# The second piece of wo as five transfers, and a small row built on GpSimd, in a decode kernel on one core

## The chip, the core and the metric

The kernel runs on one core of one Trainium2 chip. The time is device microseconds of that core for one execution. Each execution reads all inputs from HBM and writes 512 output numbers. The engines are TensorE (PE, with its weight loads as PEld), VectorE (DVE), ScalarE (ACT), GpSimd (POOL) and SyncE (SP, which issues nearly all transfers here). Sixteen DMA engines move the data.

## What is computed

One token passes through grouped-query attention with a long cache and through a gated feed-forward block; a sigmoid gate mixes the two results. All tensors are bf16. The shapes are: x 1x512, 32 query heads over 8 cache heads, 32768 cached positions of 128 numbers, feed-forward width 1792.

```python
g = _sigmoid((x * gate_w).sum(-1, keepdims=True))
# attention: q = x @ wq in 32 heads; k and v repeated 4 times
scores = jnp.einsum("bhqd,bhkd->bhqk", q, k) * (Dh ** -0.5)
p = _softmax(scores, axis=-1)
o = jnp.einsum("bhqk,bhkd->bhqd", p, v)
a = o.reshape(B, Sq, Hq * Dh) @ wo
# feed-forward: the same x
b = (_silu(x @ w_gate) * (x @ w_up)) @ w_down
return g * a + (1 - g) * b
```

The two caches are 134 MB of the 148 MB that are read; wq and wo are 4.2 MB each, and the three feed-forward matrices 1.8 MB each.

## The kernel before

**Storage.** `page` is five pages of 32 KB in each of the 128 partitions. One cache head of K or V fills two pages. wq first lies in page 3, the gate and up matrices in page 4; K uses pages 0 to 2 in turn (that of the first head 1 and 2), V pages 3 and 4, V of the last head pages 2 and 0. wo takes page 3 once V of the seventh head has been used there. Row `p` of the view of wo is partition `p`: it holds 32 rows of wo, `j` = 0 to 31, of 512 numbers (1 KB) each.

**The queue of transfers.** SP issues everything in program order (lines 310 to 329): wq, x, gate_w, gate, up, then K of head 0 in two halves, K of head 1 in two halves, V of head 0, K of head 2, V of head 1 and so on; then V of the last head in two halves, w_down, and wo. Several of these wait until a page is free: the second half of K of head 1 (line 289) waits until PE has transposed the first half of K of head 0, and wo (line 325) waits until V of the seventh head is used. What is queued behind a waiting transfer waits too. A load of 128 partitions is spread over the sixteen DMA engines, eight partitions to each.

**wo in pieces.** `WO_CUTS = [0, 16, 25, 29, 31, 32]` cuts wo by `j` into five pieces of 16, 9, 4, 2 and 1 rows per partition (2048, 1152, 512, 256 and 128 KB), each with a semaphore `sem_wo[k]`, so that PE can begin on a piece when it has landed. `emit_wo` (line 241) waits for a piece and multiplies its rows.

**The start.** PE begins with two small products (line 442) of a row of ones with `r_row`, the numbers 0 to 127 and their negatives; the difference is zero on the diagonal only, and DVE makes the identity matrix from it (line 622). `r_row` is built by DVE: a memset and seven additions (lines 606 to 614), each twice as long as the one before and each waiting for the last, and one multiplication by -1 (line 615). After line 442 PE waits for x (line 445), turns it into a column (line 448), and makes the queries (line 463) and the feed-forward products (line 501). Then the loop over the eight heads starts (line 533).

**The loop and the end.** In each turn PE transposes K in 16 units (line 337), DVE copies them out of PSUM (line 711), PE makes the scores (line 349), and the exponentials (ACT, line 586) and the product with V of the head before (line 406) follow. `emit_end` does the last head's V, the w_down product, and the first piece of wo (line 557, sixteen products at line 220). Behind the block, ACT copies their sum (line 762), PE adds it up in four column groups (line 757) and does the other four pieces of wo with `emit_rows` (line 231, four small products for each row `j`); DVE rounds the result (line 764), and two stores send it out.

**GpSimd** does two memsets of ones (lines 263 and 264), and then only adds to a semaphore (line 271) when pairs of K loads are in.

## Time and profile before

| what | value |
|---|---|
| median of 3 runs | 350.95 us (350.76 to 351.65) |
| profiled execution | 350.67 us |
| its span, first to last instruction | 349.3 us |
| mean granted clock of TensorE | 0.833 |
| PE, DVE, ACT, POOL busy | 75%, 54%, 10%, 0% of the span |
| bytes over the span | 148.11 MB read, 424 GB/s |

The profiled execution's own time is 1.37 us longer than its span. A busy PE is not a PE at its peak, since its products overlap. Three views are used: the page of the whole execution (busy time, the span in 40 slices, DMA queues, the chain of work that ended last); the instructions in order of time, where a bracket behind a row tells how long the engine idled before it and what ended that; and a table of stretches of time, with the busy time of each engine, the clock granted to TensorE and the mean busy share of the sixteen DMA engines in each.

### The profile page before, as it was taken

The page shows a single profiled execution, that of the slowest core. Times are in us where ns is not written, and L with a number is a line of the kernel's source. Part 1 is how long each engine was busy: PE and PEld are TensorE (multiplying, and loading weights), DVE is VectorE, ACT ScalarE, POOL GpSimd, SP SyncE. Part 2 cuts the span into 40 slices and gives each one's busy share as a digit, 9 for nine tenths or more (in the row PEclk, how much of TensorE's full clock was granted, in tenths as well). Part 3 has the DMA queues.
Part 4 walks back from the last instruction along what each step waited for, and adds up shares of the span by engine and source line. Part 5 has one row for each costly group of instructions (what it writes and reads, how often), then busy time and mean ns, then how long its engine had stood idle before and what let it go on. Part 6 is the DMA issues. An engine that isn't in the chain of part 4 may idle for free. (4 is left out here: it accounts for less than half of the span.)

```text
span 349.3 us, 8832 instructions
## 1 busy us (share of the span) xinstructions
PE 261.8 (75%) x3915; PEld 221.4 (63%) x3915; DVE 187.2 (54%) x236; ACT 33.4 (10%) x143; POOL 0.4 (0%) x6
## 2 busy tenths in 40 slices
PE   1354995899549980999669992999379983999484
PEld 1124994898349960997359942997279843995232
DVE  4144895698118931797139911796149811894110
ACT  1002000300210003000210003000400003000400
POOL 0000000000000000000000000000000000000000
PEclk9975898799858996799659986799859975998875
DMA  8999999999999999999999999999999999999995
GB/s 325 420 454 420 422 432 449 460 413 428 443 428 450 413 435 450 428 435 420 428 473 413 428 428 428 465 413 428 443 413 465 413 428 443 428 416 420 423 423 231
DMA packets 4051, 148.22 MB, mean 424 GB/s; under 512 B 458, under 2 KB 588, under 8 KB 844
## 3 DMA queue, kind: packets, MB, share of 16 engines
q1 hardware_dynamic: 4040, 148.12, 98.5%
q8 instruction: 6, 0.10, 0.1%
q14 instruction: 1, 0.01, 0.0%
q10 hardware_dynamic: 4, 0.00, 0.0%
HBM read 148.11 MB, written 0.00 MB: 424 GB/s over the span
## 5 line engine op out<-in xcount | busy, mean ns | idle before, releaser
L711 DVE COPY ktT<-pst 128x2048 bf16<-128x2048 bf16 x128 | 153.4, 1221 | 66.1 <-PE pst L337 62.1
L337 PE MATMUL pst<-ident_f,page 128*128 128x128 f32 x1024 | 148.7, 300 | 39.7 <-DMA page<-in_A_k_cache_dram 38.3
L337 PEld LDWEIGHTS pst<-ident_f,page 128*128 128x128 f32 x1024 | 127.2, 156 | 44.0 <-DMA page<-in_A_k_cache_dram 39.0
L349 PEld LDWEIGHTS ps_sc<-qcur,ktT 128*128 128x128 bf16 x2048 | 63.9, 97 | 8.1 <-DVE ktT L711 7.1
L349 PE MATMUL ps_sc<-qcur,ktT 128*128 128x8 bf16 x2048 | 64.2, 166 | 6.4 <-DVE ktT L711 6.4
L406 PE MATMUL ps_o<-page,ET 128*16 128x512 bf16 x512 | 38.2, 465 | 3.5 <-ACT ET L586 3.5
L406 PEld LDWEIGHTS ps_o<-page,ET 128*16 128x16 bf16 x512 | 14.1, 105 | 23.9 <-issue 12.1
L586 ACT ACTIVATE ET<-ps_sc,nbias 128x128 bf16 x64 | 23.9, 556 | 51.7 <-DVE nbias L737 51.7
L579 ACT ACTIVATE acc<-ps_o 128x512 f32<-128x512 f32 x8 | 4.8, 597 | 221.7 <-PE ps_o L406 217.6
L729 DVE TENSOR_REDUCE gm<-ps_m 4x1 f32<-4x128 f32 x8 | 2.2, 279 | 39.8 <-PE ps_m L386 39.8
L586 ACT ACTIVATION_READ_ACCUMULATOR ET<-ps_sc,nbias 128x1 f32 x64 | 18.3, 286 | 0.0
L719 DVE TENSOR_REDUCE pmaxf<-ps_sc 128x4 f32<-128x512 f32 x16 | 11.0, 686 | 8.4 <-PE ps_sc L349 8.4
L427 PE MATMUL ps_m<-sel,acc 128*128 128x4 f32 x64 | 8.4, 255 | 1.8 <-ACT acc L579 1.6
L427 PEld LDWEIGHTS ps_m<-sel,acc 128*128 128x128 f32 x64 | 7.7, 191 | 2.5 <-ACT acc L579 2.2
L390 PE MATMUL ps_m<-diag,ones_f 4*128 4x4 f32 x16 | 3.6, 294 | 6.8 <-DVE diag L733 6.8
L390 PEld LDWEIGHTS ps_m<-diag,ones_f 4*128 4x128 f32 x16 | 3.2, 245 | 8.4 <-issue 8.4
L696 DVE RECIPROCAL rS<-ps_m 128x4 f32<-128x4 f32 x9 | 1.6, 183 | 10.8 <-PE ps_m L427 10.8
L448 PE MATMUL ps_m<-ones_bf,x_row 1*128 1x1 bf16 x4 | 0.3, 172 | 9.3 <-DMA x_row<-in_A_x_dram 9.3
L418 PEld LDWEIGHTS ps_m<-esum,ones_f 128*128 128x128 f32 x32 | 4.2, 190 | 3.5 <-issue 3.5
L448 PEld LDWEIGHTS ps_m<-ones_bf,x_row 1*128 1x128 bf16 x4 | 0.2, 115 | 9.6 <-DMA x_row<-in_A_x_dram 9.6
L418 PE MATMUL ps_m<-esum,ones_f 128*128 128x4 f32 x32 | 4.9, 258 | 0.0
L764 DVE CAST res_row<-ps_sc 128x128 bf16<-128x128 f32 x1 | 0.3, 292 | 7.9 <-PE ps_sc L231 7.9
(70 smaller groups left out, 55.4 us busy)
## 6 DMA issues: line engine op xcount, KB each, us to landing
page<-in_A_k_cache_dram SPq DMA_DIRECT2D x4, 4096.0 KB, 34.4
page<-in_A_v_cache_dram SPq DMA_DIRECT2D x2, 4096.0 KB, 27.3
page<-in_A_wq_dram SPq DMA_DIRECT2D x1, 4096.0 KB, 13.5
page<-in_A_wo_dram SPq DMA_DIRECT2D x1, 2048.0 KB, 18.5
page<-in_B_w_gate_dram SPq DMA_DIRECT2D x1, 1792.0 KB, 16.7
page<-in_B_w_up_dram SPq DMA_DIRECT2D x1, 1792.0 KB, 20.6
wd<-in_B_w_down_dram SPq DMA_DIRECT2D x1, 1792.0 KB, 21.0
page<-in_A_wo_dram SPq DMA_DIRECT2D x1, 1152.0 KB, 21.0
```

What stands on the lines that cost most here:

```text
L337: ins = pe.transpose(pst[u % NST][:, k * 128 : (k + 1) * 128], kv[:, n * 128 : (n + 1) * 128], ident_f[:, :],)
L349: ins = pe.matmul(ps_sc[b][:, col : col + 2 * HPG], kt[:, k, e, :], qcur[:, e, :], start=(e == 0), stop=(e == 1),)
L390: pe.matmul(ps_m[:, M_B0 : M_B0 + HPG], ones_f[0:HPG, :], diag[:, :], start=True, stop=True,).then_inc(sem_b, STEP)
L406: ins = pe.matmul(ps_o[32 * c : 32 * c + RQ * HPG, :], ET[:, n : n + RQ, :].rearrange("p n h -> p (n h)"), v[:, k * RQ : (k + 1) * RQ, :], ...
L418: pe.matmul(ps_m[:, M_S0 : M_S0 + HPG], ones_f[:, :], esum[:, b, :], start=(b == 0), stop=(b == NB - 1),)
L427: ins = pe.matmul(ps_m[:, M_P0 : M_P0 + HPG], acc[:, q, :], sel4[:, q * HPG : (q + 1) * HPG], start=(q == 0), stop=(q == RQ - 1),)
L579: act.activation(part, ps_o[:, :], ACT.Copy).then_inc(sem_acc, STEP)
L586: act.activation(ET[:, b * R : (b + 1) * R, h], sc[:, h, bass.ds(bank, R)], ACT.Exp, bias=nbias[:, h : h + 1], scale=SCALE, accum_out=esum ...
L696: dve.reciprocal(rS[:, :], ps_m[:, M_S0 : M_S0 + HPG]).then_inc(sem_rs, STEP)
L711: dve.tensor_copy(ktT[:, n % NKT, :], pst[n % NST][:, :].bitcast(BF16)).then_inc(sem_cp, 1)
L719: dve.tensor_reduce(pmaxf[:, b, :], sc, AX.X, ALU.max).then_inc(sem_d, 1)
L729: dve.tensor_reduce(gm[:, :], ps_m[0:HPG, M_A0 : M_A0 + 128], AX.X, ALU.max).then_inc(sem_d, STEP - 2)
```

## The change

The second piece of wo (rows `j` = 16 to 24, 9 KB of each partition) becomes five transfers on the same semaphore: one of partitions 0 to 111, and four of four partitions each, 112 to 115, 116 to 119, 120 to 123 and 124 to 127. A transfer of 112 partitions gives each of sixteen DMA engines seven; one of four partitions is put on four of them. By the change's own words the same four engines take all four, so that they carry 11 rows of this piece and the other twelve 7, where each carried 8. PE waits for 80 counts in place of 16.

`r_row` is built by GpSimd, by the same nine operations, behind its two memsets; PE waits for the ninth count. In the built program one more instruction stands on GpSimd just ahead of its first addition: it loads the library of code that holds this operation. Nothing else moves on any engine.

```diff
+    ROW_CUTS = [(0, 112)] + [(n, n + 4) for n in range(112, 128, 4)]
...
         def emit_wo(pe, k):
-            pe.wait_ge(sem_wo[k], 16)
+            pe.wait_ge(sem_wo[k], 16 * len(ROW_CUTS) if k == 1 else 16)
...
             def _(pool):
                 pool.memset(ones_f[:, :], 1.0).then_inc(sem_ones, 1)
                 pool.memset(ones_bf[:, :], 1.0).then_inc(sem_ones, 1)
+                pool.memset(r_row[:, 0, 0:1], 0.0).then_inc(sem_r, 1)
+                n, k = 1, 1
+                while n < 128:
+                    pool.wait_ge(sem_r, k)
+                    pool.tensor_scalar(
+                        r_row[:, 0, n : 2 * n], r_row[:, 0, 0:n], float(n), None, op0=ALU.add
+                    ).then_inc(sem_r, 1)
+                    n *= 2
+                    k += 1
+                pool.wait_ge(sem_r, k)
+                pool.tensor_scalar(
+                    r_row[:, 1, :], r_row[:, 0, :], -1.0, None, op0=ALU.mult
+                ).then_inc(sem_r, 1)
...
                 for k, s in enumerate(sem_wo):
                     a, b = WO_CUTS[k], WO_CUTS[k + 1]
-                    sp.dma_start(wo_v[:, a:b, :], src[:, a:b, :]).then_inc(s, 16)
+                    for lo, hi in ROW_CUTS if k == 1 else [(0, 128)]:
+                        sp.dma_start(wo_v[lo:hi, a:b, :], src[lo:hi, a:b, :]).then_inc(s, 16)
...
                 def emit_start():
-                    pe.wait_ge(sem_dve_r, 1)
+                    pe.wait_ge(sem_r, 9)
...
-                dchain(dve.memset(r_row[:, 0, 0:1], 0.0))
-                n = 1
-                while n < 128:
-                    dchain(
-                        dve.tensor_scalar(
-                            r_row[:, 0, n : 2 * n], r_row[:, 0, 0:n], float(n), None, op0=ALU.add
-                        )
-                    )
-                    n *= 2
-                dve.tensor_scalar(
-                    r_row[:, 1, :], r_row[:, 0, :], -1.0, None, op0=ALU.mult
-                ).then_inc(sem_dve_r, 1)
                 dchain(dve.memset(qblk[:, :], 0.0))
```

More of the change, by code (lines that the diff above doesn't have):

```diff
@@ L94, in bass_gated_mix__gqa_block_cached__swiglu_ffn__decode_kernel @@
         sem_pz = S_("s_pz")
-        sem_dve_r = S_("s_dve_r")
+        sem_r = S_("s_r")
         sem_pe_d = S_("s_pe_d")
```

## The prediction

> **What bounds the kernel now.** First the page of the whole execution: the span, the DMA queues, the bytes.

> ```profile
> span 349.3 us, 8832 instructions
> q1 hardware_dynamic: 4040, 148.12, 98.5%
> q8 instruction: 6, 0.10, 0.1%
> q14 instruction: 1, 0.01, 0.0%
> HBM read 148.11 MB, written 0.00 MB: 424 GB/s over the span
> ```

> The data queue takes 98.5% of sixteen DMA engines over the span. No compute engine is near that, so only two things can change the time: bytes that arrive later, or the tail behind the last bytes. Seven packets are not data but instruction code (6 on q8, 1 on q14).

> Then the tail: the chain of work that ended last, and the DMA issues of wo with their time to landing.

> ```profile
> 344.52 0.61 ACT acc L762
> 345.12 0.04 issue
> 345.17 2.50 PE ps_sc L231 x72
> 347.67 0.02 issue
> 347.69 0.29 DVE res_row L764
> ```

> ```profile
> page<-in_A_wo_dram SPq DMA_DIRECT2D x1, 1152.0 KB, 21.0
> page<-in_A_wo_dram SPq DMA_DIRECT2D x1, 512.0 KB, 21.8
> page<-in_A_wo_dram SPq DMA_DIRECT2D x1, 256.0 KB, 22.0
> page<-in_A_wo_dram SPq DMA_DIRECT2D x1, 128.0 KB, 21.8
> ```

> ```profile
> L329 SPq DMA_DIRECT2D page<-in_A_wo_dram x5: 328/432/434, 323.7 to 325.5; - x5
> ```

> Issues run from 323.7 to 325.5, some 0.45 us apart, so the pieces land at about 345.1, 346.4, 347.0 and 347.3 us. Line 231 works through them to 347.67. Last, the tail in stretches of 0.2 us; the last two numbers of a row are the DMA engines' share and GB/s, the one ahead of them the granted clock.

> ```profile
> 344.60:344.80 0.20, 0.00 (x0) 0.00 (x0) 0.00 (x0) 0.20 (x1) 0.00 (x0) 0.50 1.06 405
> 345.00:345.20 0.20, 0.03 (x4) 0.04 (x5) 0.00 (x0) 0.11 (x1) 0.00 (x0) 0.50 0.78 292
> 345.20:345.40 0.20, 0.20 (x7) 0.18 (x11) 0.00 (x0) 0.00 (x0) 0.00 (x0) 0.50 0.49 190
> 346.00:346.20 0.20, 0.20 (x20) 0.20 (x12) 0.00 (x0) 0.00 (x0) 0.00 (x0) 0.50 0.38 138
> 346.40:346.60 0.20, 0.20 (x20) 0.20 (x13) 0.00 (x0) 0.00 (x0) 0.00 (x0) 0.50 0.32 108
> 346.60:346.80 0.20, 0.20 (x20) 0.20 (x15) 0.00 (x0) 0.00 (x0) 0.00 (x0) 0.50 0.12 41
> ```

> The share falls in two steps: to about half by 345.3, then it stays near 0.4 until 346.6. So some nine engines are done 1.3 to 1.5 us before the other seven, and a piece counts as landed when the last of the sixteen has put its part down. Seven late engines and seven packets of code fit each other: an engine that fetches code in mid-stream stays behind to the end, since all do equal work. Which engines are late no view tells.

> **The change, part by part: wo.** One row of the second piece on one engine: 1152 KB at 424 GB/s take 2.78 us, for eight rows on each engine, so 0.35 us a row. An engine with 7 rows is done 0.35 us earlier, in this piece and in the three behind it. One with 11 is done 3 x 0.35 = 1.05 us later.

> If the four are among the early nine, they end 1.05 us behind the early group, still at or before the late seven, who come 0.35 us earlier: the last piece lands at about 346.95 in place of 347.3. Of these 0.35 us PE can use only what it waits for:

> ```profile
> L231 PEld LDWEIGHTS ps_sc<-page,O 128*32 128x32 bf16 x64 | 1.8, 142 | 0.3 <-DMA page<-in_A_wo_dram 0.2
> ```

> Of its idle time 0.2 us was ended by a wo transfer. Otherwise it was busy from 345.17 on, at a granted clock of 0.50, and it started there because of line 762, that is of the first piece, which isn't touched. So the gain is between 0 (another engine is last) and 0.2 us; I take 0.15, since the row is rounded and PE's own pace is next behind it. If the tail's clock were full, up to 0.35 would come.

> SP issues four transfers more, 4 x 0.43 = 1.7 us from the same row. Ahead of the last data stand some 20 us of landing time, so nothing runs dry: 0. It costs something only if that queue were shorter than 4 us. The higher count on the semaphore moves no other wait on PE.

> Four transfers of 36 KB could each have a fixed price. The last piece, 128 KB, lands 0.45 + 21.8 - 22.0 = 0.25 us behind the one before (rounding makes it 0.15 to 0.4), and at 424 GB/s it takes 0.31. So a small transfer in a full queue costs at most 0.1 us more than its bytes: 0 to 0.4 us for four, nearest 0, which I take. [...]

> **The change: r_row on GpSimd.** DVE loses nine operations; its two PSUM memsets start some 1.7 us earlier, and nobody waits for them early. What matters is when r_row is ready. In order of time:

> ```profile
> 0.73 1.28 ACT L568 ACT_TABLE_LOAD   x1 [0.73 <-PEq L782]
> 0.87 0.10 POOL L264 MEMSET ones_bf<- 128x2 bf16 x1
> 0.89 1.34 DVE L610 TENSOR_SCALAR r_row<-r_row 1x1 f32<-1x1 f32 x7
> 1.17 0.32 SPq L311 DMA_DIRECT2D x_row<-in_A_x_dram  x1
> 2.53 0.79 PE L442 MATMUL ps_sc<-ones_f,r_row 1*128 1x128 f32 x2 [2.53 <-DVE r_row L615]
> 3.12 0.63 PE L442 MATMUL ps_sc<-r_row,ones_f 1*128 1x128 f32 x2
> 13.07 0.29 PE L448 MATMUL ps_m<-ones_bf,x_row 1*128 1x1 bf16 x4 [9.33 <-DMA x_row<-in_A_x_dram]
> 22.83 3.16 PE L501 MATMUL pst<-page,xT 128*1 128x448 bf16 x32 [1.79 <-DMA page<-in_B_w_up_dram]
> 44.66 0.33 SPq L290 DMA_DIRECT2D page<-in_A_k_cache_dram  x1
> ```

> Line 442 runs from 2.53 to 3.75, then PE idles 9.33 us for x. So r_row may be ready up to 13.07 - 1.22 = 11.8 us and nothing moves. Up to 1.8 us later line 501's wait for the up matrix takes it. Beyond that the first transposes come late, and with them the K load of 44.66, which they release. How much data is queued then:

> ```profile
> page<-in_A_k_cache_dram SPq DMA_DIRECT2D x1, 4096.0 KB, 17.1
> ```

> That load lands 17.1 us after its issue; its own bytes take 4096 KB / 424 GB/s = 9.9, so 7.2 are queue and start. Less 1.0 from issue to first data (the first transfer is issued at 0.73; the rows of the first two microseconds below) and less the 1.4 us by which early engines run ahead, some 5 us are spare.

> ```profile
> 0.00:1.00 1.00, 0.00 (x0) 0.00 (x0) 0.17 (x2) 0.27 (x1) 0.44 (x6) 1.00 0.00 0
> 1.00:2.00 1.00, 0.00 (x0) 0.00 (x0) 0.83 (x6) 1.00 (x1) 0.00 (x0) 1.00 1.34 360
> ```

> So r_row costs bytes only from about 11.8 + 1.8 + 5 = 18.6 us on, one for one.

> When is it ready? GpSimd is free at 0.97. DVE's chain steps every 0.19 us (1.34 / 7). GpSimd's step isn't in the trace; its memset of 0.10 us against DVE's 0.06 for a still smaller one speaks for about double, 0.4, and eight steps are 3.2 us. The load of code is not in the trace either. Bounds: 0, were the code there already, and 11.9 us, what a 1 KB transfer takes behind full queues (x: issued at 1.17, awaited at 13.07). Nearest in kind is ACT's load of a table, 1.28 us. Ready at 0.97 + 1.28 + 3.2 = 5.5 us, bounds 2.5 and 16.1: each of these below 18.6. I take 0. [...]

> **Sum.** wo -0.15, the rest 0: the profiled execution of 350.67 us (1.37 of it outside the span) would be 350.52. It stood 0.28 below the median of 350.95, so the median is put at 350.8.

> **The rivals.** (a) One of the four engines is late already. Then its 11 rows, not the seven rows of the rest, set the last landing. It decides from any lag over about 0.2 us behind the early group (1.05 + 0.2 is where the late seven now land, less 0.15 that PE absorbs), and lags are 1.3 to 1.5 or none. Price: the last landing 0.4 to 1.05 us later, as it is the first or last of the seven, and the tail behind it at full length: 351.35 to 352.0, middle 351.7. For it: seven of sixteen are late, and four drawn blindly would all be early in only some 7 of 100 cases. Against: code fetches that follow one another need not be spread blindly; if they sit side by side, four early neighbours are as likely as not.

> (b) r_row is later than 18.6 us, because its code needs two trips behind full queues, 2 x 11.9 us: ready at 0.97 + 23.8 + 3.2 = 28, so 9 us of missing DMA, 360. For it: x shows what a trip under load costs. Against: one trip is hidden, and the seven packets of code took 0.1% of the DMA engines between them.

> (c) The change doesn't do what it says: the four small transfers go to different engines, every engine is back at eight rows, 350.95.

> (d) The code of GpSimd comes through the same DMA engines as more packets like the seven, and DVE's shorter program saves one. A late engine hit twice adds 1.4 us: 352.3. One late engine fewer gains nothing while six remain.

> (e) A fixed price for small transfers, 0.4 us at its upper bound, on the four engines: inside the slack of early engines, so 350.95; this is a term of (a) more than a case.

> **How the numbers follow.** Forecast 0.45, (a) 0.30, (b) 0.10, (c) with (e) 0.07, (d) 0.08. This kernel's measurement tells a change from none at about 0.3%, 1.05 us: the forecast, (c) and most of (a) are inside it. Slower by more: (b) 0.10, (d) 0.06, and 0.12 of (a) for its upper end plus what (b) might add in small: 0.28. Faster by more needs the whole tail gap of 1.4 us to close, or a tail at full clock: 0.05. Within: 0.67. The range runs from 350.4 (0.35 gained and 0.2 of spread) to 352.3 (the top of (a), and (d)); it leaves out (b) and little else.

> **What would show it.** The granted clock near 0.50 in the tail, the DMA share keeping its first level longer and ending 0.3 us earlier, and PE's idle time for wo in line 231 gone: right. If the share has a long low foot at 4 engines or fewer, lasting past 347.3, (a) is so. GpSimd's additions should end before 11.8 us with PE still waiting for x; a DMA share well under 1 around 50 us would mean (b). More than seven instruction packets mean (d). Wrong I would be, above all, over which engines are late, since no view of before names them.

## The result and the profile after

The changed kernel takes 355.85 us (median of five runs, 355.17 to 356.53); the kernel before, run beside it, 350.83 us. The ratio is 1.0141, with a 95% interval of 1.0129 to 1.0153: 5.0 us slower, where 350.8 us had been forecast. The profiled execution of the changed kernel took 356.18 us, 5.51 more than that of the kernel before.

The page of the whole execution, the same rows as before:

```profile
span 354.9 us, 8838 instructions
q1 hardware_dynamic: 4056, 148.12, 98.4%
q8 instruction: 6, 0.10, 0.1%
q14 instruction: 1, 0.01, 0.0%
HBM read 148.11 MB, written 0.00 MB: 417 GB/s over the span
```

The bytes are the same, and so are the seven packets of code. The DMA engines are busy for the same share of a span that is 5.6 us longer. So they are busy longer with the same work. The chain of work that ended last shows where the end comes from (start, duration, what):

```profile
325.24 27.27 DMA page<-in_A_wo_dram
352.51 0.04 issue
352.55 0.66 PE ps_sc L232 x12
353.22 0.02 issue
353.24 0.29 DVE res_row L767
```

In the kernel before, 2.50 us of PE's products stood here without a gap, and DVE's rounding began at 347.69. Now PE has only twelve products left when the last transfer of wo lands at 352.51, and DVE begins at 353.24, 5.55 us later. The DMA issues of wo, with the size and the time to landing where the view has one, first in the changed kernel:

```profile
page<-in_A_wo_dram SPq DMA_DIRECT2D x1, 2048.0 KB, 21.3
page<-in_A_wo_dram SPq DMA_DIRECT2D x1, 1008.0 KB
page<-in_A_wo_dram SPq DMA_DIRECT2D x1, 512.0 KB, 27.0
page<-in_A_wo_dram SPq DMA_DIRECT2D x1, 256.0 KB, 27.3
page<-in_A_wo_dram SPq DMA_DIRECT2D x4, 36.0 KB
page<-in_A_wo_dram SPq DMA_DIRECT2D x1, 128.0 KB, 27.1
```

and the first piece in the kernel before:

```profile
page<-in_A_wo_dram SPq DMA_DIRECT2D x1, 2048.0 KB, 18.5
```

The three pieces behind the cut one needed 21.8 to 22.0 us before and need 27.0 to 27.3 now. The first piece, which isn't cut and is queued ahead of the cut one, is late as well, 21.3 us in place of 18.5. Part of that is an earlier issue; SP's issues of wo in the changed kernel, in order of time:

```profile
322.62 3.53 SPq L344 DMA_DIRECT2D page<-in_A_wo_dram  x9
```

They begin at 322.62, before at 323.67, so that the first piece lands at 343.9 in place of 342.2, 1.75 us later. The stretches of 2 us show how the engines spend this time. In each row the first numbers are the busy times of PE, PE's loads, DVE, ACT and GpSimd; the last three are the granted clock, the share of time in which the sixteen DMA engines are busy, and GB/s. A packet counts whole in the stretch in which it starts, so that a share can pass 1. The kernel before:

```profile
338.00:340.00 2.00, 1.39 (x18) 0.53 (x17) 0.98 (x5) 0.00 (x0) 0.00 (x0) 1.00 0.99 420
340.00:342.00 2.00, 0.00 (x0) 0.00 (x0) 0.00 (x0) 0.00 (x0) 0.00 (x0) 1.00 0.96 401
342.00:344.00 2.00, 1.67 (x16) 0.41 (x16) 0.00 (x0) 0.00 (x0) 0.00 (x0) 0.55 0.98 405
344.00:346.00 2.00, 1.04 (x28) 0.78 (x28) 0.00 (x0) 0.60 (x1) 0.00 (x0) 0.50 0.75 288
```

and the changed kernel:

```profile
338.00:340.00 2.00, 0.42 (x7) 0.10 (x1) 0.44 (x3) 0.00 (x0) 0.00 (x0) 1.00 0.98 415
340.00:342.00 2.00, 0.00 (x0) 0.00 (x0) 0.00 (x0) 0.00 (x0) 0.00 (x0) 0.74 1.08 263
342.00:344.00 2.00, 0.00 (x0) 0.00 (x0) 0.00 (x0) 0.00 (x0) 0.00 (x0) 0.50 0.99 198
344.00:346.00 2.00, 1.88 (x16) 0.40 (x16) 0.00 (x0) 0.00 (x0) 0.00 (x0) 0.50 0.99 183
346.00:348.00 2.00, 0.66 (x8) 0.20 (x8) 0.00 (x0) 0.60 (x1) 0.00 (x0) 0.50 0.97 133
348.00:350.00 2.00, 0.00 (x0) 0.00 (x0) 0.00 (x0) 0.00 (x0) 0.00 (x0) 0.50 0.94 226
350.00:352.00 2.00, 1.28 (x44) 1.01 (x48) 0.00 (x0) 0.00 (x0) 0.00 (x0) 0.50 0.36 134
```

The third row of each is the one to learn from. At equal busy share (0.98 and 0.99) the engines move 405 GB/s before and 198 after. The DMA engines hardly wait for work; the rows that they carry take longer. The trace also holds a record of every packet, which no view prints, and these say the same. A packet of 9 KB is one row of the second piece, one of 16 KB a row of the first piece. In ns:

```
                    9 KB rows of the second piece    16 KB rows of the first piece
before              347 to 359, mean 353             612 to 621
after               347 to 1306, median 695          612 to 1209
```

And PE waits longer for wo (engine, line, what it waited for: total us, times, longest). The kernel before:

```profile
PE ps_sc L220 <- DMA page<-in_A_wo_dram: 2.8, 1, 2.8
PEld ps_sc L231 <- DMA page<-in_A_wo_dram: 0.2, 1, 0.2
```

and the changed kernel:

```profile
PE ps_sc L221 <- DMA page<-in_A_wo_dram: 5.5, 1, 5.5
PEld ps_sc L232 <- DMA page<-in_A_wo_dram: 4.4, 4, 3.6
PE ps_sc L232 <- DMA page<-in_A_wo_dram: 3.1, 1, 3.1
```

The other half of the change did what was forecast. The start of the changed kernel, in order of time:

```profile
0.92 0.09 POOL L266 MEMSET r_row<- 1x1 f32 x1
1.09 2.27 POOL L270 TENSOR_SCALAR r_row<-r_row 1x1 f32<-1x1 f32 x7
3.44 0.53 POOL L276 TENSOR_SCALAR r_row<-r_row 1x128 f32<-1x128 f32 x1
4.03 0.79 PE L457 MATMUL ps_sc<-ones_f,r_row 1*128 1x128 f32 x2 [4.03 <-POOL r_row L276]
12.89 0.29 PE L463 MATMUL ps_m<-ones_bf,x_row 1*128 1x1 bf16 x4 [7.65 <-DMA x_row<-in_A_x_dram]
```

`r_row` is ready at 3.97 us, and PE still idles 7.65 us for x behind it.

### The profile page after: what moved, and what is told of

The parts are those of the page before. It is cut to its first block, busy times and chain, and to the rows that moved or that the text cites. A ratio compares the mean times of both kernels' runs of the same rounds, so it can differ in the third digit from the quotient of the medians.

```text
span 354.9 us, 8838 instructions
## 1 busy us (share of the span) xinstructions
PE 264.7 (75%) x3915; PEld 222.2 (63%) x3915; DVE 186.4 (53%) x227; ACT 33.4 (9%) x143; POOL 2.8 (1%) x15
## 3 DMA queue, kind: packets, MB, share of 16 engines
q1 hardware_dynamic: 4056, 148.12, 98.4%
HBM read 148.11 MB, written 0.00 MB: 417 GB/s over the span
## 4 chain that ended last, share of the span: by engine, by line
DMA 61%; PE 34%; issue 2%; DVE 1%; SPq 1%; DVEq 0%
DMA page<-in_A_k_cache_dram 54%; PE pst L352 26%; DMA page<-in_A_wo_dram 8%; PE ps_sc L364 6%; PE ps_o L421 1%; DVE ktT L714 1%; SPq L344 1%; SPq L328 0%; DVE pmaxf L722 0%; PE ps_sc L232 0%; PE ps_m L405 0%; PE ps_m L401 0%; SPq L324 0%; SPq L325 0%; DVE res_row L767 0%
## 5 line engine op out<-in xcount | busy, mean ns | idle before, releaser
L352 PEld LDWEIGHTS pst<-ident_f,page 128*128 128x128 f32 x1024 | 128.0, 156 | 40.5 <-DMA page<-in_A_k_cache_dram 35.5
L421 PE MATMUL ps_o<-page,ET 128*16 128x512 bf16 x512 | 39.9, 479 | 3.6 <-ACT ET L601 3.5
L442 PE MATMUL ps_m<-sel,acc 128*128 128x4 f32 x64 | 8.4, 255 | 1.8 <-ACT acc L594 1.6
L442 PEld LDWEIGHTS ps_m<-sel,acc 128*128 128x128 f32 x64 | 7.7, 191 | 2.5 <-ACT acc L594 2.2
L221 PE MATMUL ps_sc<-page,O 128*1 128x512 bf16 x16 | 1.9, 621 | 5.5 <-DMA page<-in_A_wo_dram 5.5
## 6 DMA issues: line engine op xcount, KB each, us to landing
page<-in_A_k_cache_dram SPq DMA_DIRECT2D x4, 4096.0 KB, 34.4
page<-in_A_v_cache_dram SPq DMA_DIRECT2D x2, 4096.0 KB, 27.1
page<-in_A_wq_dram SPq DMA_DIRECT2D x1, 4096.0 KB, 13.5
page<-in_A_wo_dram SPq DMA_DIRECT2D x1, 2048.0 KB, 21.3
wd<-in_B_w_down_dram SPq DMA_DIRECT2D x1, 1792.0 KB, 20.3
```

Of the source, the lines that this page charges most:

```text
L352: ins = pe.transpose(pst[u % NST][:, k * 128 : (k + 1) * 128], kv[:, n * 128 : (n + 1) * 128], ident_f[:, :],)
L421: ins = pe.matmul(ps_o[32 * c : 32 * c + RQ * HPG, :], ET[:, n : n + RQ, :].rearrange("p n h -> p (n h)"), v[:, k * RQ : (k + 1) * RQ, :], ...
L442: ins = pe.matmul(ps_m[:, M_P0 : M_P0 + HPG], acc[:, q, :], sel4[:, q * HPG : (q + 1) * HPG], start=(q == 0), stop=(q == RQ - 1),)
```

## The experiments

Medians and ratios to the kernel before, run beside each (its medians lay near 350.8, in the run of eight transfers of 16 rows at 351.46):

| run | us | ratio, 95% interval |
|---|---|---|
| gpsimd_row_alone | 350.72 | 1.0003 (0.9993 to 1.0013) |
| wo_cut_alone | 355.79 | 1.0139 (1.0122 to 1.0156) |
| wo_112_and_16 | 355.10 | 1.0122 (1.0105 to 1.0138) |
| wo_five_full_width | 350.99 | 1.0005 (0.9996 to 1.0015) |
| spare_4x4_one_port | 353.31 | 1.0072 (1.0055 to 1.0088) |
| spare_4x4_own_ports | 351.42 | 1.0021 (1.0011 to 1.0030) |
| wo_64_and_64 | 354.34 | 1.0099 (1.0082 to 1.0116) |
| wo_112_and_16_near | 355.12 | 1.0120 (1.0103 to 1.0137) |
| wo_eight_of_16 | 355.17 | 1.0100 (1.0067 to 1.0132) |
| tail_own_groups | 351.44 | 1.0016 (1.0007 to 1.0026) |
| tail_other_groups | 352.78 | 1.0057 (1.0040 to 1.0074) |
| tail_one_group | 352.08 | 1.0040 (1.0027 to 1.0052) |
| alone_own_groups | 361.24 | 1.0295 (1.0278 to 1.0312) |
| alone_other_groups | 361.34 | 1.0301 (1.0284 to 1.0318) |
| alone_one_group | 369.80 | 1.0558 (1.0528 to 1.0588) |

### Which half of the change

`gpsimd_row_alone` is the changed kernel with wo as it was; `wo_cut_alone` is the kernel before with only wo cut.

> Only the row of numbers is moved to GpSimd; wo is loaded as before. Three theories put the loss of 5.0 us into wo (paths: engines that write into the same group of partitions slow each other; uneven: an engine with 11 rows is the last one; number: each further transfer has a price). All three expect 350.8 us here, within 1 us. The theory that GpSimd is to blame expects 355.8 us.

> Only the second piece of wo is cut (112 rows and four times 4 rows); DVE builds the row of numbers. Paths, uneven and number expect the whole loss, 355.8 us, and the first piece of wo, which isn't cut, landing some 1.8 us late as in the changed kernel (343.9 against 342.2 us). GpSimd to blame: 350.8 us.

The row on GpSimd costs nothing (1.0003), the cut costs all of it (1.0139 alone, 1.0141 with the row). Its 9 KB rows took 717 ns on average, against 353 in the run with the row on GpSimd alone, and its first piece landed 20.3 us behind the issue, against 18.5.

### Uneven engines, the number of transfers, or the partitions

The first of these runs is to give each engine eight rows again but keeps the cut at partition 112. The second makes five transfers too, but cuts along `j`, so that each has all 128 partitions. The diffs from here on show the deciding lines only; the higher count for which PE waits, and the loop over `ROW_CUTS` where there is one, are as in the change.

```diff
+    ROW_CUTS = [(0, 112), (112, 128)]
```

```diff
-                    sp.dma_start(wo_v[:, a:b, :], src[:, a:b, :]).then_inc(s, 16)
+                    for c, d in [(16, 18), (18, 20), (20, 22), (22, 24), (24, 25)] if k == 1 else [(a, b)]:
+                        sp.dma_start(wo_v[:, c:d, :], src[:, c:d, :]).then_inc(s, 16)
```

> The second piece of wo as 112 rows and 16 rows, two transfers, eight rows for each of the sixteen engines as before. Paths: the seven rows of an engine no longer lie in the group of partitions that it has to itself, so most of the loss stays; an estimate in which a row takes 0.35 us alone and 0.70 us where two engines write to one group gives +4.2 us, 355.0 us (range 353.5 to 356.5), and a first piece that lands late. Uneven: every engine has eight rows, so 350.8 us. Number: one further transfer of the four, +1.3 us, 352.1 us.

> The second piece of wo as five transfers of all 128 partitions (two, two, two, two and one row of each partition) in place of the one. Number: five transfers cost as much as in the changed kernel, 355.8 us. Paths and uneven: each engine keeps its own eight partitions, 350.8 us, within 0.5 us.

Stretches of 5 us of the first,

```profile
340.00:345.00 5.00, 0.62 (x9) 0.27 (x12) 0.19 (x1) 0.00 (x0) 0.00 (x0) 0.79 1.02 228
```

and of the second:

```profile
340.00:345.00 5.00, 1.88 (x16) 0.40 (x16) 0.00 (x0) 0.39 (x1) 0.00 (x0) 0.62 0.99 375
```

Both have busy DMA engines, but 228 and 375 GB/s. Equal engines cut at 112 are 4.3 us slower than before, with rows of 649 ns on average; so uneven engines are not the main cause (they would leave 0.7 us, 355.79 against 355.10). Five transfers of full width cost 0.2 us together, and nothing that the interval tells from zero; so the number of transfers isn't either. What is left of the three is which partitions are written together.

### The same four small transfers, with other partitions

Here the second piece is one full transfer again, and the four small transfers are added to it, into a spare page. They differ only in the partitions. In the first kernel each small transfer takes four neighbours (by the theory one group, written by four engines at once). In the second it takes every fourth partition, which the author takes for the own groups of the four engines; no view shows which engine writes them. The diff is that of the first; the second has `rows = slice(t, 16 + t, 4)`. In both PE waits for all five transfers before it begins on the second piece, and 144 KB more are read than before.

```diff
+                    if k == 1:
+                        spare = page[:, PG_F, 0 : WOJ * NOUT].rearrange("p (j n) -> p j n", j=WOJ)
+                        for t in range(4):
+                            rows = slice(112 + 4 * t, 116 + 4 * t)
+                            sp.dma_start(spare[rows, a:b, :], src[rows, a:b, :]).then_inc(s, 16)
```

> The second piece of wo in one transfer of 128 partitions, and behind it the four small transfers of the change once more, partitions 112 to 115, 116 to 119 and so on, into a page that is free by then (their data isn't used; PE waits for all five). Each of the four engines carries 12 rows, 147 KB or 0.35 us are read besides. Paths: the four engines of a small transfer write into one group of four neighbouring partitions and queue there, an estimate with a row at 0.35 us alone gives +4.1 us, 354.9 us (range 353.5 to 356.5), but the first piece lands as before, at 342.2 us, since nothing is cut ahead of it. Uneven: four rows more, 4 x 0.35 = 1.4 us at most, 350.8 to 352.2 us.

> [...] Paths: no two engines meet, so only four rows more on four engines: 350.8 us if all four are early ones, up to 352.2 us if one is late. A price for small transfers or for four engines as such: the same as with neighbouring partitions, about 355 us.

Stretches with neighbours,

```profile
340.00:345.00 5.00, 1.88 (x16) 0.41 (x16) 0.00 (x0) 0.49 (x1) 0.00 (x0) 0.58 1.03 329
345.00:350.00 5.00, 2.50 (x68) 1.57 (x68) 0.00 (x0) 0.10 (x1) 0.00 (x0) 0.50 0.61 161
```

and with every fourth partition:

```profile
340.00:345.00 5.00, 1.87 (x16) 0.41 (x16) 0.00 (x0) 0.53 (x1) 0.00 (x0) 0.58 0.98 403
345.00:350.00 5.00, 3.04 (x72) 1.68 (x72) 0.29 (x1) 0.07 (x1) 0.00 (x0) 0.50 0.22 83
347.20:347.60 0.40, 0.40 (x16) 0.17 (x8) 0.00 (x0) 0.00 (x0) 0.00 (x0) 0.50 0.05 18
```

Number of transfers, bytes and rows are equal, and the times differ by 1.9 us. With every fourth partition all rows of 9 KB took 347 to 359 ns; with neighbours up to 1211. This is the cleanest proof that the partitions matter. The last row shows the plain price of uneven engines: a share of 0.05 is about one engine of sixteen, busy alone after the others are done, and the whole costs 0.7 us.

The packet records also show how far the slowdown reaches. All packets in flight at 344.00 us, each against the mean time of its size in the kernel before:

```
with every fourth partition      17 rows      0.98 to 1.02 times
with neighbours                  16 rows      2.3 to 3.5 times
```

With neighbours every row is slow, six rows of the full transfer behind among them. At most four of the sixteen belong to the small transfers, and at most four groups are visited, so at least eight engines were slow that by the theory had their group to themselves. Writing into neighbours sets the loss off (353.31 us against 351.42), but it is not confined to the engines that share a group by the theory. How it spreads, no run shows.

### Two transfers of 64 partitions, reads, and eight transfers of 16

Two transfers of 64 partitions are to give each engine four rows; if these are neighbours, two engines by the theory always share a group. The next kernel keeps the cut at 112 but reads the piece from one contiguous block of wo (so its second piece holds the wrong rows of wo), to see whether the reads are slow. The third cuts the piece into eight transfers of 16 partitions, which the author took to put four engines to a group. No view shows either.

```diff
+    ROW_CUTS = [(0, 64), (64, 128)]
```

```diff
+                        if k == 1:
+                            near = A_wo[0 : 128 * (b - a), :].rearrange("(p j) n -> p j n", j=b - a)
+                            sp.dma_start(wo_v[lo:hi, a:b, :], near[lo:hi, :, :]).then_inc(s, 16)
```

```diff
+    ROW_CUTS = [(n, n + 16) for n in range(0, 128, 16)]
```

> The second piece of wo as two transfers of 64 partitions, four rows on each engine in either. Paths: each half has eight of the sixteen groups, so two engines write to each group throughout; a row then takes 0.70 in place of 0.35 us, eight rows 2.8 us more: 353.6 us (range 352.8 to 354.6) if an engine takes neighbouring partitions, 358 us if it takes every sixteenth. Uneven and number: 350.8 us.

> As 112 and 16 rows, but the second piece is read from the first 1.2 MB of wo, where the 9 KB of one partition follow those of the one before (a partition's 9 KB stood 32 KB apart); wo's rows 16 to 24 of each partition are then the wrong ones. Were the reads from HBM to blame, the time would move well away from the 355.1 us of 112 and 16 rows, to about 350.8 us at best. Paths into the partitions: 355.1 us, within 1 us, since the writes are the same.

> The second piece of wo as eight transfers of 16 partitions, one row of 9 KB on each engine in each. [...] Paths: by the estimate with which 112 and 16 rows were put at 355.0 us (measured 355.1), +7.0 us, 357.8 us (range 356 to 361); more than any run before, though each engine has eight rows and there are no small counts of engines. Uneven and number: 350.8 to 351.2 us.

The stretch of the run with twice 64 partitions:

```profile
340.00:345.00 5.00, 1.28 (x16) 0.40 (x16) 0.00 (x0) 0.00 (x0) 0.00 (x0) 0.50 1.00 228
```

Again the engines are busy throughout and move half. The run costs 3.6 us, its rows took 661 ns on average. Other places in HBM change nothing (355.12 and 355.10), which speaks for the writing side. The eight transfers are a miss: 357.8 had been estimated for four engines that share a group in step, within 356 to 361, and 355.17 came. Their rows took 640 ns, no longer than those of 112 and 16 (649) or of twice 64 (661). So in the full stream a row took nearly twice its time in all three cuts, however many engines share a group by the theory, which a plain sharing of each group does not give.

### A rival: the distance from the own group

A second theory fits most of this: a row may be slow merely because it goes to partitions that are not the engine's own. Three runs put the four small transfers behind all of wo: into every fourth partition from 0, into every fourth from 64, and into neighbours from 112. The author takes these for own groups, for other groups, which belong to four other engines, and for one group at a time; the runs bear these names, and no view shows which engine writes where. The diff is that of own groups; the others have `slice(64 + t, 80 + t, 4)` and `slice(112 + 4 * t, 116 + 4 * t)`. Four engines are to carry four rows more each. PE waits for the four transfers before the last piece.

```diff
+                spare = page[:, PG_F, 0 : WOJ * NOUT].rearrange("p (j n) -> p j n", j=WOJ)
+                for t in range(4):
+                    rows = slice(t, 16 + t, 4)
+                    sp.dma_start(spare[rows, 16:25, :], src[rows, 16:25, :]).then_inc(sem_wo[4], 16)
```

> All pieces of wo in one transfer each, and behind the last one four small transfers of 9 KB rows into a free page (their data isn't used; PE waits for all). [...] Each has 4 x 0.35 = 1.4 us more to do, alone at the end. Both theories below: the four engines end at about 347.2 us, one late engine among them at 348.0, PE has no product left but those of the last piece: 351.4 us, as in the run where these transfers stood behind the second piece.

> [...] Paths (engines slow each other only where two write into one group at the same time): as with own groups, 351.4 us, within 0.5 us. Distance (an engine is slow whenever it writes outside its own group, whether another is there or not): rows take 0.70 in place of 0.35 us, +1.4 us, 352.8 us or more.

> As the two runs before, but partitions 112 to 115, 116 to 119 and so on, as in the change: the four engines of a small transfer write into one group. Paths: a group passes one row in 0.35 us, sixteen rows 5.6 us if the engines keep step, less by what they drift apart (the same four transfers behind the second piece cost 2.6 us where 4.1 were estimated): 353 to 355 us. Distance: as with other groups.

Two of the three missed. Other groups took 352.78, where sharing let expect 351.4; neighbours took 352.08, below the 353 to 355 of sharing. The run with other groups hits what distance gave, but it does not separate the two theories. The late engines were still writing their last pieces until 347.81 us (346.88 with own groups), and 54 of the 128 rows of 1 KB took 60 to 124 ns in place of 46. These rows are of a full transfer, so engines that write at home were slowed too, which distance can't do. Eight such rows belong to each engine, so at least seven engines were slowed, more than the four whose groups are visited by the theory; here too the slowdown spreads. The last three rows of the run with neighbours took 348 to 358 ns, as in a full transfer. The runs with own and with other groups also read rows that lie equally far apart in HBM, so the spacing of the reads does not make their difference.

So the same three were run with nothing else in flight: SP waits for the last piece of wo, then issues four transfers of 32 KB rows, and waits for them (512 KB more than the kernel before reads). The slices are the same three.

```diff
+                sp.wait_ge(sem_wo[4], 16)
+                spare = page[:, PG_F, 0 : WOJ * NOUT].rearrange("p (j n) -> p j n", j=WOJ)
+                for t in range(4):
+                    rows = slice(t, 16 + t, 4)
+                    sp.dma_start(spare[rows, :, :], src[rows, :, :]).then_inc(sem_spare, 16)
+                sp.wait_ge(sem_spare, 64)
```

> SP waits until all of wo has landed and then issues four small transfers of four whole partition rows (32 KB each) into a free page; nothing else is being moved. [...] A row takes 2 x 0.614 = 1.23 us by the 16 KB rows of the first piece, four rows 4.9 us; with about 1.4 us from issue to data and 0.4 to landing, the block ends some 354 us after the start and the last products follow: 360 us (range 359 to 362). The same by both theories; this is the measure for the two beside it.

> [...] Paths (slow only where two engines write into one group at the same time): the same time as with own groups, within 0.7 us, rows of 1.23 us. Distance (an engine is slow outside its own group): rows of 2.4 us, +4.9 us.

> As the run with own groups, but partitions 112 to 115, 116 to 119 and so on: all four engines of a transfer in one group. Paths: the first rows take up to 4.9 us; if the engines then keep step, 19.6 us for all (+14.7 us), if they drift apart to one group each, 4.9 + 3 x 1.23 = 8.6 us (+3.7 us): from +3.7 to +14.7 us over the run with own groups. Distance: the same as with other groups.

A wait of SP for these transfers, and a stretch, with own groups,

```profile
SPq L261 <- DMA page<-in_A_wo_dram: 5.1, 1, 5.1
350.00:352.00 2.00, 0.00 (x0) 0.00 (x0) 0.00 (x0) 0.00 (x0) 0.00 (x0) 0.50 0.32 115
```

with other groups,

```profile
SPq L261 <- DMA page<-in_A_wo_dram: 4.8, 1, 4.8
350.00:352.00 2.00, 0.00 (x0) 0.00 (x0) 0.00 (x0) 0.00 (x0) 0.00 (x0) 0.50 0.31 131
```

and with one group at a time:

```profile
SPq L261 <- DMA page<-in_A_wo_dram: 14.6, 1, 14.6
350.00:352.00 2.00, 0.00 (x0) 0.00 (x0) 0.00 (x0) 0.00 (x0) 0.00 (x0) 0.50 0.51 66
```

The partitions from 64 on cost nothing when nothing else is in flight: 361.34 and 361.24 us, with sixteen rows of 1368 and 1406 ns on average (the quickest 1213 in both, the first ones up to 1913 and 1855). If they are foreign, as the author takes them, the theory of distance falls. Neighbours are 8.6 us slower with the same bytes, where distance had 4.9: their sixteen rows took 1526 to 4644 ns, 3079 on average, 2.2 times as long as with own groups. The stretch shows it in small: a higher share, 0.51 (four rows that start there, counted whole), and half the bytes, 66 GB/s.

## Why the prediction was wrong

**The row on GpSimd: right.** The forecast was ready at 5.5 us, and without effect up to 11.8. It was ready at 3.97, since the load of code cost next to nothing here (the first addition starts 0.08 us after the memset ends) and a step took 2.27 / 7 = 0.32 us, not 0.4. Both terms were too high, and the limit was far enough away. Whether the code lay there from an earlier execution, no run tells.

**wo: wrong.** The term was -0.15 us and measured +5.0. The step that failed is "An engine with 7 rows is done 0.35 us earlier, in this piece and in the three behind it. One with 11 is done 3 x 0.35 = 1.05 us later." It counts rows and takes for granted that a row costs 0.35 us on whichever engine, into whichever partitions. The 0.35 was right for a full transfer (353 ns on average). In the piece cut at partition 112 a row took 695 ns in the median. By the theory the cut deals the partitions out anew: if the rows go to the engines as blocks of neighbours, seven neighbours straddle the groups that a full transfer keeps apart, and four neighbours put four engines into one group. No view shows this dealing.

The packet records let this be added up. A packet that begins as another ends is taken for the same engine, though no view names it. Then the second piece makes twelve chains of seven rows and four of eleven, as the change says, and the first piece in the kernel before sixteen chains of eight. The chain that ends last is one of eleven. It began on the piece at 341.66 us, as the late engines did before (341.10 to 341.77), and its rows took 8.4 us. Eight rows at 0.35 took 2.8 there before, and eleven would take 3.9. So about 1.05 of the 5.6 us are the uneven count, as forecast for a late engine, and 4.5 are slow rows. Behind the piece this chain took 2.28 us to its last row at 352.36, as long as the last rows took before.

The first piece was hit as well: early engines begin on the cut piece while late ones are still at the first, and 15 of its 128 rows took over 625 ns, up to 1209, in place of at most 621. Its last row ended at 342.61 in place of 341.77, 0.84 us later; the rest of the 1.75 us lies between the last row and the landing, and no run explains it. Where the second piece stayed full width and the small ones came behind it, as in `spare_4x4_one_port`, the first piece landed no later than with own groups (19.6 us in both). That fits; it was not tested by a run of its own.

A simple sum, in which engines share a group's 0.35 us a row equally and the rows go to the engines in blocks of neighbours, rests on the groups that the author assumed. It gave +4.2 us for the cut into 112 and 16 (measured +4.3) and +2.8 for twice 64 (+3.6). For the neighbours in the spare page it gave +4.1 (+2.6) and +7.0 for eight times 16 (+3.7, by the interval 2.4 to 4.6). It confines the slowdown to the groups that are shared, which the packet records contradict, so the near hit on 112 and 16 is in part luck.

**The small price for small transfers: right.** At 0 to 0.4 us for four, taken as 0; five transfers in place of one cost 0.2 us at full width.

**Rival (a), one of the four is late: true, and hidden.** In the run with own groups a single engine ends last, and the price there is 0.7 us, within the 0.4 to 1.05 given. In the changed kernel the chain of eleven rows that ends last ends 1.17 us behind all others (352.36 against 351.19). That is about a fifth of what came. **(b)** did not happen. **(c)** is out, since four chains carry eleven rows and twelve carry seven. **(d)** is out: there are six and one packets of code, as before. **(e)** is the small price above.

One of the signs listed shows the gap. "A long low foot" was expected for a late engine; it came, from about 351 us on, but behind some ten microseconds in which the share stayed near 1 while the bytes halved. The prediction had no case in which DMA engines are busy and slow. Its range reached to 352.3 only because the rivals inside it counted rows or packets, and none asked to which partitions an engine writes.

**What stays open.** Why engines that by the theory share with nobody are slowed as well, and why a row in the full stream took some 1.8 to 1.9 times its time whether by the theory two or four engines share a group, while the neighbours of the quiet run took 2.2 times. Which partitions make a group, and how a transfer of 112, 64 or 16 partitions is dealt out, was assumed; the times fit it in part, and no view shows it. That the writes and not the reads are slow is argued from runs in which the reads differ, and no run isolates it. Nor is it known which engines fetch code, or whether that makes one late; one of the four is late.

No version was found that beats the kernel before: the row on GpSimd without the cut is the same in time.

## What to carry to other kernels

Cut a load along the free dimension, so that each piece has all 128 partitions (five such transfers in place of one cost 0.2 us here); the cut along the partitions about doubled the time of its rows (353 ns to 695 in the median) and slowed some of a transfer queued ahead of it (15 of 128 rows, up to 1209 ns in place of 621). In a table of stretches, read the DMA engines' share and GB/s together: a share near 1 with half the bytes (0.99 at 198 GB/s, where 0.98 had moved 405) meant here that the rows were slow, and equal rows for all engines did not cure it (355.10 us with 112 and 16). Before moving rows between engines, ask which partitions will be written at the same time (neighbours or every fourth partition made 1.9 us here).

## What the runs showed of the hardware that was not expected

With the second piece cut along the partitions a row took nearly twice its time in the full stream: 353 ns to 661 with two transfers of 64 partitions, 649 with 112 and 16, 640 with eight of 16. With nothing else in flight, transfers of four neighbours took 2.2 times as long for a row as transfers of every fourth partition (1406 ns to 3079 on average); every fourth partition from 64 was as quick as every fourth from 0 (361.34 and 361.24 us).

Rows of full transfers are slowed as well: all sixteen rows in flight at 344.00 us took 2.3 to 3.5 times their time in the run with neighbours in the spare page, and at most four of the sixteen were of the small transfers.

GpSimd's first library operation began 0.08 us behind the memset before it, although the instruction that loads its code stands between them; next to nothing of the 0 to 11.9 us that had been allowed for it was needed in this execution.
